# Local attention with channel mix: straight weight reads and every second PSUM column in the first unit's fp32 products

## The chip, the cores and the metric

The kernel runs on one core of one Trainium2 chip. The metric is the device time of one execution in microseconds (us). Before the change it is 390.84 us, the median of three runs (390.59 to 391.21).

## The reference

A local attention (chunks of 32 queries, each with 56 neighbouring keys and 8 memory keys, 4 batches, 8 heads, 768 positions, 64 values a head) is followed by a channel mix. Only the second part is touched by the change; its input `x` is the attention's output with 512 features per token.

```python
def _moe_ref(x, mu_k, mu_r, w_k, w_v, w_r):
    x_prev = ...                       # x, shifted by one token
    xk = mu_k * x + (1.0 - mu_k) * x_prev
    xr = mu_r * x + (1.0 - mu_r) * x_prev
    k = np.maximum(xk @ w_k, 0.0)      # 512 -> 1024
    v = k * k @ w_v                    # 1024 -> 512
    r = 1.0 / (1.0 + np.exp(-(xr @ w_r)))   # 512 -> 512
    return (r * v).astype(np.float32)
```

## The kernel before

The 4 x 768 tokens are cut into 12 units of 256 tokens, numbered `u`, and each unit into two tiles of 128 tokens, numbered `c`. For a unit the matrix engine (TensorE, in the profile PE) computes the scores `s`, transposes the probabilities into `pt`, multiplies them with the values into `px`, and then does the three products of the channel mix: `ph` (with `w_k`), the gate `pr` (with `w_r`) and `pv` (with `w_v`). The vector engine (DVE) and the scalar engine (ACT) do everything between the products.

The weights come from memory as 64-bit words in chunks `w0` to `w9` (`raw`). ACT and DVE turn each into a single fp32 tile `w` (`f_abs`, `f_low`, `f_join`: L325, L328, L332), and later split that into a high and a low part of type fp32r, `wk`, `wr` or `wv` and `wl` (L271 or L273, and L345). From unit 1 on each product is a sum of three fp32r products: high x high, high x low, low x high (L952, L1026, L1125). The first unit comes while the weights are still on their way; there the products use the undivided fp32 tiles, without a split:

- `f_row` (L998): `ph` of unit 0, 256 or 128 columns a call;
- `f_gate` with `is_whole(u)` (L943): `pr` of unit 0, for each of the two tiles four calls of 512 columns;
- `f_s2` with `is_whole(u, half)` (L1112): the first half of the sum over the 1024 features in `pv` of unit 0, four calls of 512 columns for each tile. The second half of this sum is done in fp32r (L1125), into the same PSUM bank.

A call with fp32 operands stands in the profile as two matmul rows with a weight load each, so L943 has 2 x 4 x 2 = 16 rows and L1112 as many. What is called the weight in these products, `w`, is the streamed operand of TensorE; the activations (`xf`, `kf`) are loaded into the array.

The order on each engine is set ahead of time by a planner (`Plan`) from a table of costs (`PE_COST`, `FULL`, `BLOCK`) and due times (`te_order`), and issued in that order. Loads and stores are issued from the queue of the sync engine (SP).

The columns of `w_v` and `w_r` lie in memory sorted: first the 256 even columns, then the 256 odd ones (`paired`, on the host). Two helpers put them back in order in the product:

```python
def woven(a):
    return a.rearrange("p (t n) -> p n t", t=2)

def pairs(a):
    return a.rearrange("p (n t) -> p n t", t=2)
```

With `woven(w)` the streamed operand is read alternately from the two halves: element 0, 256, 1, 257 and so on. With `pairs(p)` the results go to columns 0, 1, 2, 3 and so on, side by side. `f_row` uses neither: it reads its columns and writes them straight through.

Of the kernel before, what the change touches and what calls it, by code (L numbers as in the profile page):

```python
# [16 lines left out]
P = 128  # L17
# [8 lines left out]
FT = DFF // P  # L26
# [23 lines left out]
def woven(a):  # L50

    return a.rearrange("p (t n) -> p n t", t=2)


def pairs(a):
    return a.rearrange("p (n t) -> p n t", t=2)
# [22 lines left out]
class Plan:  # L81
# [7 lines left out]
    def op(self, alts, fn, deps=(), new=(), use=(), due=1e9):  # L89
        fixed = isinstance(alts, tuple)  # L90
        if fixed:
            alts = [alts]
        o = Op([(a + (False,))[:3] for a in alts], fn, deps, new, use, due)
        o.seq, o.fixed = len(self.ops), fixed
        self.ops.append(o)
        return o
# [121 lines left out]
def local_attention__then__channel_mix(  # L218
# [22 lines left out]
    def sb(tag, shape, name, dt=F32):  # L241
        return work.tile(shape, dt, tag=tag, name=name, bufs=bufs.get(tag, 1))

    def ps(tag, name, n=1):
        return psA.tile([P, n * 512], F32, tag=tag, name=name, bufs=bufs[tag])
# [21 lines left out]
    T = {}  # L267
# [109 lines left out]
    def wdeps(hl, ks):  # L377
        return [o for k in ks for o in wdone[id(hl[0]), k]]

    def word_deps(hl, ks):  # L380
        return [whole[id(hl[0]), k][0] for k in ks], [whole[id(hl[0]), k][1] for k in ks]

    def is_whole(u, half=0):
        return u == 0 and half == 0
# [550 lines left out]
    def channel_mix(u):  # L935
        b, t0 = units[u]

        def f_gate(c):
            p = T["pr", u, c] = ps("m", f"pr{u}_{c}")
            if is_whole(u):  # L940
                for k in range(KT):
                    w = T["w", id(wr_hl[0]), k // 2][:, k % 2 * DM : (k % 2 + 1) * DM]
                    nc.tensor.matmul(  # L943
                        pairs(p), T["xf", u, 1][:, k, c * P : (c + 1) * P], woven(w),
                        start=(k == 0), stop=(k == KT - 1),
                    )
                return
            xh, xl = T["xh", u, 1], T["xl", u, 1]
            wh, wl = ([w[k // 2][:, k % 2 * DM : (k % 2 + 1) * DM] for k in range(KT)] for w in wr_hl)
            for k in range(KT):  # L950
                for n, (x, w) in enumerate(((xh, wh[k]), (xh, wl[k]), (xl, wh[k]))):
                    nc.tensor.matmul(  # L952
                        pairs(p), x[:, k, c * P : (c + 1) * P], woven(w),
                        start=(k + n == 0), stop=(k == KT - 1 and n == 2),
                    )
# [13 lines left out]
        for c in range(QPU):  # L969
            grp.append(  # L970
                op(
                    ("pe", FULL if is_whole(u) else BLOCK), lambda c=c: f_gate(c),
                    grp[-1:] + (list(mix[u, 1][0].values()) if is_whole(u) else list(mix[u, 1][:2])) + wr,
                    new=[gs[c]], use=list(mix[u, 1][2:]) + wr_use, due=due["g", u, c],
                )
            )
# [41 lines left out]
        for f in range(FT // 2):  # L1018
# [14 lines left out]
            if f % 2 == 0:  # L1033
                kf = Slot(f"kf{z}")
# [64 lines left out]
        for c in range(QPU):  # L1099
            s = Slot("m")  # L1100
            prev = None
            for half in range(2):
                fs = range(FT // 4 * half, FT // 4 * (half + 1))

                def f_s2(c=c, half=half, fs=fs):
                    if half == 0:
                        T["pv", u, c] = ps("m", f"pv{u}_{c}")
                    p = T["pv", u, c]
                    if is_whole(u, half):
                        for f in [2 * f2 + i for f2 in fs for i in range(2)]:  # L1110
                            w = T["w", id(wv_hl[0]), f // 2][:, f % 2 * DM : (f % 2 + 1) * DM]
                            nc.tensor.matmul(  # L1112
                                pairs(p), T["kf", u, f // 4][:, f % 4, c * P : (c + 1) * P], woven(w),
                                start=(f == 0), stop=False,
                            )
                        return
                    for f2 in fs:
                        for i in range(2):
                            f = 2 * f2 + i
                            wh, wl = (w[f2][:, i * DM : (i + 1) * DM] for w in wv_hl)  # L1120
                            kh = T["kh", u, f2][:, i]
                            kl = T["kl", u, f2][:, i]
                            tc_ = slice(c * P, (c + 1) * P)
                            for n, (x, w) in enumerate(((kh, wh), (kh, wl), (kl, wh))):
                                nc.tensor.matmul(  # L1125
                                    pairs(p), x[:, tc_], woven(w), start=(f + n == 0), stop=(f == FT - 1 and n == 2)
                                )

                deps, use = [prev], []
                for f in fs:  # L1130
                    deps += ks[f][:2]
                    use += ks[f][2:]
                if is_whole(u, half):
                    wd, wd_use = word_deps(wv_hl, fs)
                    deps += wd
                    use += wd_use
                else:
                    deps += wdeps(wv_hl, fs)
                dv = due["v", u, c, half]
                prev = op(("pe", FULL if is_whole(u, half) else BLOCK), f_s2, deps, new=[s] if half == 0 else [], use=use + ([s] if half else []), due=dv)  # L1140
                if u == 0:
                    first_v.append(prev)
                if u == FAST - 1:
                    last_v.append(prev)

            def f_o(c=c):
                o = T["o", u, c] = sb("o", [P, DM], f"o{u}_{c}")
                p, sg = T["pv", u, c], T["sg", u][:, c * DM : (c + 1) * DM]
                nc.vector.tensor_mul(o, p, sg)

            def f_st(c=c):
                nc.sync.dma_start(out[b, t0 + c * P : t0 + (c + 1) * P, :], T["o", u, c])

            os = Slot("o")
            o_o = op(("dve", 0.62), f_o, [prev, o_g[c]], new=[os], use=[s, sgs], due=dv + BLOCK + 2)
            op(("dma", 0.75), f_st, [o_o], use=[os], due=dv + BLOCK + 6)
# [16 lines left out]
    with tc.manual_schedule():  # L1173
        for o in plan.order():
            if o.eng == "pe":
                n = 0 if ("ph", 0, 0) in T else int((o.start - busy - 0.2) / (0.43 if busy else 0.86))
# [56 lines left out]
```

## Time and profile before

| what | value |
|---|---|
| median of three runs | 390.84 us (390.59 to 391.21) |
| the profiled execution | 390.65 us |
| span of its profile | 388.5 us |
| busy DVE, ACT | 319.1 us (82%), 221.4 us (57%) |
| rows of L943 and L1112 | 16 and 16, 700 to 803 ns each |
| where they stand | 33.2 to 53.6 us of the span |

PE is the matrix engine, PEld its weight loads, SPq the queue from which transfers are issued. A matmul row's length is modelled and reaches into the next row, so what a row costs in a stream of rows is the distance of its start from the next one's start. In rows of the timeline the first number is the start, the second the length, both in us; in brackets behind a row stands how long its engine had been idle and what ended that.

### The profile page before, as it was taken

To read this page: it belongs to the slowest core of one execution; us is meant where nothing else is said; L and a number is where in the kernel's file an instruction comes from. 1 tells how busy PE (TensorE), PEld (TensorE's weight loads), DVE (VectorE), ACT (ScalarE), POOL (GpSimd) and SP (SyncE) were. 2 spreads that over 40 slices of the span, in tenths; PEclk is the share of its full clock that TensorE was granted. 3 is DMA by queue.
4 is the path that set the end of the run, shared out by engine and by line. 5 is a ranking of instruction groups with operands and counts; after the bars stand their busy time and mean duration, and the time that the engine had idled before them with its cause. 6 is when DMAs were issued, how large, how long until landed. Compare 5 with 4: busy or idle time off the path is not lost.

```text
span 388.5 us, 10736 instructions
## 1 busy us (share of the span) xinstructions
PE 382.2 (98%) x4776; PEld 351.8 (91%) x4776; DVE 319.1 (82%) x510; ACT 221.4 (57%) x329; POOL 2.8 (1%) x13
## 2 busy tenths in 40 slices
PE   8899999999999999999999999999999999999996
PEld 6785469988999999999999999999999999999996
DVE  3989798999899699699699689789779869969264
ACT  1789764955654464465466376267267356568260
POOL 2000000000000000000000000000000000000000
PEclk9999999999999999999999999999999999999999
DMA  8999683050042144134134134124134120000101
GB/s 318 420 392 417 251 280 128 29 164 29 27 158 118 54 126 149 54 114 162 54 112 164 57 110 164 56 110 164 56 108 167 56 87 24 30 29 2 54 2 54
DMA packets 13053, 48.98 MB, mean 126 GB/s; under 512 B 1488, under 2 KB 1872, under 8 KB 12496
## 3 DMA queue, kind: packets, MB, share of 16 engines
q1 hardware_dynamic: 13008, 48.31, 33.4%
q8 instruction: 37, 0.61, 0.7%
q14 instruction: 8, 0.07, 0.1%
HBM read 42.01 MB, written 6.29 MB: 124 GB/s over the span
## 4 chain that ended last, share of the span: by engine, by line
PE 97%; DVE 1%; issue 0%; ACT 0%; DVEq 0%
PE ph L1026 31%; PE pr L952 15%; PE accy L856 10%; PE accz L856 7%; PE accx L856 7%; PE px L526 6%; PE s L429 4%; PE pv L1125 4%; PE ph L998 4%; PE pt L509 3%; PE pv L1112 2%; PE pr L943 2%; PE warm L1179 1%; DVE mx L442 0%; DVE e L447 0%
## 5 line engine op out<-in xcount | busy, mean ns | idle before, releaser
L1026 PE MATMUL ph<-xh,wk 128*128 128x256 f32 x352 | 98.4, 280 | 0.0
L1026 PE MATMUL ph<-xl,wk 128*128 128x256 f32 x352 | 96.8, 275 | 0.0
L1026 PE MATMUL ph<-xh,wl 128*128 128x256 f32 x352 | 96.8, 275 | 0.0
L1045 ACT ACTIVATE kf<-ph 128x512 f32<-128x512 f32 x48 | 28.6, 598 | 75.9 <-PE ph L1026 75.8
L1026 PEld LDWEIGHTS ph<-xh,wk 128*128 128x128 f32 x352 | 67.5, 192 | 0.7
L1026 PEld LDWEIGHTS ph<-xl,wk 128*128 128x128 f32 x352 | 67.6, 192 | 0.1
L1026 PEld LDWEIGHTS ph<-xh,wl 128*128 128x128 f32 x352 | 67.6, 192 | 0.0
L273 DVE COPY aTz<-pt 64x512 f32<-64x512 f32 x20 | 13.8, 692 | 28.3 <-PE pt L509 19.1
L952 PE MATMUL pr<-wr,xh 128*128 128x512 f32 x88 | 34.5, 392 | 0.0
L801 DVE TENSOR_TENSOR al<-kf,ah 128x512 fp32r<-128x512 f32 x50 | 33.5, 684 | 0.4
L952 PE MATMUL pr<-wl,xh 128*128 128x512 f32 x88 | 33.4, 379 | 0.0
L952 PE MATMUL pr<-wr,xl 128*128 128x512 f32 x88 | 33.4, 379 | 0.0
L453 ACT ACTIVATE e<-e 128x1024 f32<-128x1024 f32 (+1 forms) x13 | 12.9, 993 | 33.1 <-DVE e L447 33.0
L526 PEld LDWEIGHTS px<-aTz,vw 128*64 128x64 f32 x768 | 23.5, 138 | 4.2 <-issue 1.8
L526 PE MATMUL px<-aTz,vw 128*64 128x64 f32 x768 | 25.2, 224 | 1.1 <-issue 1.1
L271 ACT CAST ah<-kf 128x512 fp32r<-128x512 f32 x40 | 24.9, 623 | 1.8 <-DVE kf L779 1.2
L1052 ACT ACTIVATE kf<-kf 128x512 f32<-128x512 f32 x40 | 25.2, 632 | 0.9
L271 ACT CAST xh<-df 128x1024 fp32r<-128x1024 f32 x11 | 16.4, 1491 | 14.6 <-DVE df L617 14.6
L856 PE MATMUL accx<-wv,ah 128*128 128x256 f32 x80 | 22.0, 275 | 0.0
L856 PE MATMUL accx<-wl,ah 128*128 128x256 f32 x80 | 22.0, 275 | 0.0
L856 PE MATMUL accx<-wv,al 128*128 128x256 f32 x80 | 22.0, 275 | 0.0
L961 ACT ACTIVATE sg<-pr 128x512 f32<-128x512 f32 x24 | 14.4, 609 | 10.6 <-PE pr L952 10.5
(125 smaller groups left out, 945.0 us busy)
## 6 DMA issues: line engine op xcount, KB each, us to landing
qk<-in_qk_dram SPq DMA_DIRECT2D x24, 768.0 KB, 5.9
vw<-in_vw_dram SPq DMA_DIRECT2D x24, 512.0 KB, 4.9
out_dram<-o SPq DMA_DIRECT2D x23, 256.0 KB, 2.0
raw<-in_w_k_dram SPq DMA_DIRECT2D x4, 1024.0 KB, 12.6
raw<-in_w_v_dram SPq DMA_DIRECT2D x4, 1024.0 KB, 8.9
raw<-in_w_r_dram SPq DMA_DIRECT2D x2, 1024.0 KB, 7.8
out_dram<-o SPq DMA_DIRECT2D x2, 128.0 KB, 1.7
id_sb<-in_ident_dram SPq DMA_DIRECT2D x1, 64.0 KB, 5.6
```

Of the source, the lines that this page charges most:

```text
L271: e.copy(dst, src)
L429: nc.tensor.matmul(s5[CHUNK * j : CHUNK * (j + 1), h, d - c, r, :], q4[z, r, j, :], k4[z, r, j, :], start=True, stop=True,)
L526: nc.tensor.matmul(p3[64 * h : 64 * h + 64, 2 * g : 2 * g + 2, CHUNK * j : CHUNK * j + CHUNK], v[:, g, h, j, :], a[:, h, g, j, :], start=True,
L801: nc.vector.tensor_sub(low(n), place[n](), T["ah", u, n].bitcast(F32))
L856: nc.tensor.matmul(o, x, w, start=(n in fresh and c + i == 0), stop=(c == cs[-1] and i == 2), skip_group_check=True)
L952: nc.tensor.matmul(pairs(p), x[:, k, c * P : (c + 1) * P], woven(w), start=(k + n == 0), stop=(k == KT - 1 and n == 2),)
L961: nc.scalar.activation(sg, p, AF.Sigmoid)
L998: nc.tensor.matmul(p[:, i * UTOK + c * P : i * UTOK + (c + n) * P], T["w", id(wk_hl[0]), k][:, fc], T["xf", u, 0][:, k, z], start=(i + k + ...
L1026: nc.tensor.matmul(pairs(p[:, i * UTOK : (i + 1) * UTOK]), w[:, fc], x[:, :, k].rearrange("p t n -> p n t"), start=(k + n == 0), stop=(k = ...
L1045: e.activation(part(), p, AF.Relu)
L1052: e.activation(q, q, AF.Square)
L1125: nc.tensor.matmul(pairs(p), x[:, tc_], woven(w), start=(f + n == 0), stop=(f == FT - 1 and n == 2))
```

## The change

Two helpers are added. `halves` reads an operand's first 256 columns and then its other 256, that is straight through. `apart` addresses the result's columns 0, 2, 4 up to 510 and then 1, 3, 5 up to 511. The two fp32 products of unit 0 that used `pairs` and `woven` use these instead. The result is the same at each column, since both sides are permuted alike.

```diff
+def halves(a):
+    return a.rearrange("p (t n) -> p t n", t=2)
+
+
+def apart(a):
+    return a.rearrange("p (n t) -> p t n", t=2)
...
                     nc.tensor.matmul(
-                        pairs(p), T["xf", u, 1][:, k, c * P : (c + 1) * P], woven(w),
+                        apart(p), T["xf", u, 1][:, k, c * P : (c + 1) * P], halves(w),
                         start=(k == 0), stop=(k == KT - 1),
                     )
...
                             nc.tensor.matmul(
-                                pairs(p), T["kf", u, f // 4][:, f % 4, c * P : (c + 1) * P], woven(w),
+                                apart(p), T["kf", u, f // 4][:, f % 4, c * P : (c + 1) * P], halves(w),
                                 start=(f == 0), stop=False,
                             )
```

A third place in the diff only breaks a line. The order of the instructions is the same on every engine before and after; behind the new helpers the line numbers grow by eight (L943 becomes L951, L1112 becomes L1120).

More of the change, by code (lines that the diff above doesn't have):

```diff
@@ L1125, in f_s2 @@
                                 nc.tensor.matmul(
-                                    pairs(p), x[:, tc_], woven(w), start=(f + n == 0), stop=(f == FT - 1 and n == 2)
+                                    pairs(p), x[:, tc_], woven(w),
+                                    start=(f + n == 0), stop=(f == FT - 1 and n == 2),
                                 )
```

## Prediction

> **What bounds the kernel now.** I read the page's first two parts first, for the busy engines, then the chain that ended last.
>
> ```profile
> PE 382.2 (98%) x4776; PEld 351.8 (91%) x4776; DVE 319.1 (82%) x510; ACT 221.4 (57%) x329; POOL 2.8 (1%) x13
> PEclk9999999999999999999999999999999999999999
> PE 97%; DVE 1%; issue 0%; ACT 0%; DVEq 0%
> ```
>
> The matrix engine (PE) is busy for 382.2 of 388.5 us, its granted clock is full in every slice, and 97% of the chain is PE work. A busy PE can still be a PE that waits now and then, so I read next what PE waited for, over the whole span. These are all rows of that view:
>
> ```profile
> PE warm L1179 <- DVE zero_sb L260: 1.2, 1, 1.2
> PE px L526 <- issue: 1.1, 2, 0.6
> PE s L429 <- issue: 0.3, 1, 0.3
> PE pt L509 <- DVE e L463: 0.2, 1, 0.2
> ```
>
> The waits sum to 2.8 us. A matmul that gets shorter therefore shortens the kernel, as long as what follows it on PE has its inputs early enough. I checked this below, because the edited matmuls run early (33 to 54 us), where the vector engine (DVE) is busy too.
>
> Third, the stage itself: pieces of the chain in order of time (start, length, what).
>
> ```profile
> 21.78 7.10 PE ph L998 x32
> 29.67 3.65 PE ph L998 x16
> 33.32 8.64 PE pr L943 x16
> 41.96 0.87 PE pt L509 x8
> 42.83 4.32 PE pv L1112 x8
> 47.15 2.02 PE px L526 x64
> 49.16 4.51 PE pv L1112 x8
> 53.68 1.41 PE s L429 x89
> 55.09 5.38 PE pv L1125 x24
> 79.45 2.59 PE pv L1125 x12
> ```
>
> The pieces touch one another: there is no hole on PE from 21.78 to 60.47 us. The edited lines are L943 (16 rows) and L1112 (8 + 8 rows). Their busy time is no price, since pipelined matmuls overlap (a row is shown with 703 ns below), so I price by spacing: 8.64 / 16 and 4.32 / 8 both give **0.540 us** for one row. The piece of 4.51 us is the same with a slower first row behind px.
>
> **The change part by part.** It moves nothing: the engines' instructions stand in the same order before and after, and the planner's costs are untouched. The 32 rows remain 32 rows with the same weights and the same 512 columns. Only two address patterns differ: the streamed operand is read straight through, and the result goes to every second PSUM column, first the even and then the odd ones.
>
> ```profile
> L943 PE MATMUL pr<-w,xf x16: 700/703/703, 33.2 to 41.3; 128*128 128x512 f32 x16
> L1112 PE MATMUL pv<-w,kf x16: 701/703/803, 42.7 to 53.0; 128*128 128x512 f32 x16
> L998 PE MATMUL ph<-xf,w x80: 275/379/483, 17.1 to 32.9; 128*128 128x256 f32 x48, 128*128 128x128 f32 x32
> ```
>
> *The read.* What does a row cost when an fp32 operand is read straight? L998 shows it: it is fp32, reads straight and writes side by side, with 256 columns. The difference of its two pieces removes the first row's start: (7.10 - 3.65) / 16 = 0.2156 us for 256 columns. Two such make 512 columns: **0.431 us**. The edited rows take 0.540, so the alternating read appears to cost 0.109 us each. The alternating read does not cost everywhere: L1125 reads alternately too, but in fp32r, and does 512 columns in 2.59 / 12 = 0.216 us, half of what straight fp32 takes per column. So the cost, if it is the read's, belongs to fp32 only. In the Trainium skill, "SBUF — State Buffer", section Specifications (TRN2), each crossing to a new 16-byte line pays. By that rule L1125 would have to be slow as well, which its 0.216 us contradicts, while L1112 fits it; I therefore do not build on the rule.
>
> *The write.* No row of this trace writes every second column, so the price has to be bounded. From below: two times L998 is the straight fp32 rate and 2 x 0.216 = 0.432 us is twice the fp32r rate. The two agree, and no row here does fp32 faster; the floor is 0.431 us. From above: adjacent columns share an aligned pair of words. L1125 writes 512 side-by-side columns in 0.216 us, which is one new pair every 0.84 ns. The new fp32 rows at 0.431 us would write one column every 0.84 ns, each in a new pair: exactly the rate of new pairs that PSUM takes from L1125 already. If instead fp32 goes over all columns twice at the fp32r rate, it asks for a new pair every 0.42 ns, twice of what any row shows, and a row could take 2 x 0.431 = 0.862 us. I take the floor, 0.431, since the pair rate that it needs is one that the trace shows and the other is not needed unless fp32 runs as two full sweeps.
>
> *The sum.* 32 x (0.540 - 0.431) = 3.49 us less on PE: 1.74 in L943, 0.87 in each half of L1112.
>
> *What is late next.* Work that stands behind the edited rows now starts up to 3.49 us sooner. Its inputs come from DVE and ACT, so I read when they are ready.
>
> ```profile
> 37.28 1.21 DVE L463 TENSOR_TENSOR e<-e,sum 128x1024 f32<-128x1024 f32 x1
> 38.41 2.35 DVE L332 SCALAR_TENSOR_TENSOR w<-w,raw 128x1024 uint32<-128x1024 uint32 x2
> 42.87 0.68 DVE L273 COPY aTz<-pt 64x512 f32<-64x512 f32 x1 [2.10 <-PE pt L509]
> 56.38 1.53 DVE L633 TENSOR_TENSOR xl<-xf,xh 128x1024 fp32r<-128x1024 f32 x1
> 60.50 0.69 DVE L1149 TENSOR_TENSOR o<-pv,sg 128x512 f32<-128x512 f32 x1 [0.86 <-PE pv L1125]
> 66.18 1.22 DVE L457 TENSOR_REDUCE sum<-e 128x16 f32<-128x1024 f32 x1 [0.69 <-ACT e L453]
> 70.21 1.22 DVE L633 TENSOR_TENSOR xl<-df,xh 128x1024 fp32r<-128x1024 f32 x1
> 71.34 1.22 DVE L345 TENSOR_TENSOR wl<-w,wr 128x1024 fp32r<-128x1024 f32 x1
> ```
>
> The transposes (pt) would start at 41.96 - 1.74 = 40.22 and need e, ready at 38.49. The first L1112 row would start at 41.1 and needs the weight joins, over at 40.76 (both of them; its first two rows use only the earlier). DVE itself stood idle for 2.10 us until pt came, so its work behind 42.87 also moves, by 1.74 us. At 60.50 it waited for pv, and at 66.18 for the exp of ACT:
>
> ```profile
> 63.18 0.60 ACT L1045 ACTIVATE kf<-ph 128x512 f32<-128x512 f32 x1 [7.89 <-PE ph L1026]
> 60.41 0.28 PE L1026 MATMUL ph<-xl,wk 128*128 128x256 f32 x1
> 72.33 0.38 PE L952 MATMUL pr<-wr,xl 128*128 128x512 f32 x1
> 73.41 0.38 PE L952 MATMUL pr<-wl,xh 128*128 128x512 f32 x1
> ```
>
> The first use of xl (60.41) has 60.41 - 57.91 = 2.50 us in hand now; with PE 3.49 ahead and DVE 1.74 ahead 0.75 is left. Thereafter DVE finds pv and exp ready sooner (ACT waited 7.89 us for PE alone, so it moves with PE) and gains the 0.86 and up to the 0.69: it is about 1.74 + 0.86 + 0.69 = 3.29 ahead. The next tight places are unit 1's gate: xl is ready at 71.43 for the row at 72.33 (0.90 in hand), wl at 72.56 for the row at 73.41 (0.85). Those need DVE at least 3.49 - 0.85 = 2.64 ahead, and it is 3.29. So I charge no wait. The queries for the scores at 53.68 would be wanted at 50.2; the transfers in this stage (one digit a microsecond, from 20 to 60 us) run dry well before that:
>
> ```profile
> DMA  9999999999999999999999994100078798587998
> 33.80 6.21 SPq L404 DMA_DIRECT2D qk<-in_qk_dram  x2
> ```
>
> The two loads were issued by 40.01 and the DMA engines fall idle at 46. From there on PE waits for nothing, so it carries the whole 3.49 us to the end. The profiled execution took 390.65 us, 2.15 more than its span and 0.19 below the median 390.84: 390.65 - 3.49 = **387.2 us**.
>
> **The rivals.** *PSUM takes the scattered writes more slowly than the read gains* (slower). For: no row shows such a write, and contiguous fp32r proves only a pair every 0.84 ns. The place is the same 32 rows, and the point from which it decides is a row of 0.540 us, a new pair every 1.05 ns. With one fp32r step (0.216 / 512 = 0.42 ns) more per column a row takes 0.431 + 0.216 = 0.647: +32 x 0.107 = +3.4, 394.1 us. With every column at double price (0.862), +32 x 0.322 = +10.3, 401.0 us. Against: fp32 needs two fp32r steps for each column, so the write has time for a new pair. The rule for this rival stands in the Trainium skill, "PSUM — Partial Sum Buffer", section Specifications (TRN2): lines of 8 bytes, and any pattern that is not contiguous slows matmuls significantly. No trace of this case shows it yet, nor whether it holds for fp32's slower columns. *The read order is not what costs* (no change). L998 differs from the edited lines in more than the read: 256 columns, not 512, and its calls change the bank while L943 stays on one for eight rows. If one of these makes the 0.540, or if the writes cost just what the read gave, the time stays at 390.65. Against: L1125 holds one bank with 512 columns and shows no loss. *DVE falls behind.* If DVE gained only the 1.74 us, the rows at 72.33 and 73.41 would wait 0.85 to 0.9 and the time would be 388.1; what I read of its idle times speaks against it.
>
> **How the numbers follow.** Forecast 387.2: chance 0.60, its own range 386.7 (an edited row a little below the floor, as a start is paid once for 512 columns) to 388.2 (DVE late). No change: 0.13. Slower: 0.27, about half of it near 394.1 and half near 401. The range from 386.7 to 394.4 holds the first two and the milder half of the third, 0.86; leaving the milder half out too would leave 0.27 outside. Within 0.2% (0.8 us) is about what a measurement of this kernel cannot tell from no change: faster 0.61, same 0.12, slower 0.27.
>
> **What would show it.** In the changed kernel's chain the pr piece with 16 rows at about 33.3 us should take 6.9 us in place of 8.64 and the two pv pieces about 3.5; the matmul rows should fall from 703 to near 594 ns. Rows above 703 ns make the scattered write the cost; rows at 703 say the read was not. PE's waits should still sum to about 2.8 us; a new row under them with DVE's xl or wl makes DVE the next bound. If the edited rows become shorter and the time does not, my reading of the slack is wrong.

## The result and the profile after

| | before | after |
|---|---|---|
| median | 391.05 us (6 runs, 390.59 to 391.57) | 387.60 us (6 runs, 387.16 to 388.02) |
| ratio | | 0.9912, 95% interval 0.9899 to 0.9925 |
| profiled execution, its span | 390.65 us, 388.5 us | 388.02 us, 385.9 us |

The kernel is 3.45 us faster by the medians, 0.9%. The page after the change shows the same machine at work: PE is busy for 98%, at full granted clock, and the chain is PE again.

```profile
PE 379.8 (98%) x4776; PEld 352.5 (91%) x4776; DVE 318.7 (83%) x510; ACT 221.5 (57%) x329; POOL 2.8 (1%) x13
PE 97%; DVE 1%; issue 0%; ACT 0%; DVEq 0%
```

What PE waited for over the whole span, after the change, again in full. Nothing new has come; the row for `s` at the start is gone.

```profile
PE warm L1188 <- DVE zero_sb L268: 1.2, 1, 1.2
PE px L534 <- issue: 1.1, 2, 0.6
PE pt L517 <- DVE e L471: 0.2, 1, 0.2
```

The stage itself, as pieces of the chain in order of time (start, length, what). L951 and L1120 are the edited lines, L1006 is `f_row`.

```profile
18.11 3.77 PE ph L1006 x32
22.67 7.10 PE ph L1006 x32
30.56 3.65 PE ph L1006 x16
34.21 6.87 PE pr L951 x16
41.95 3.44 PE pv L1120 x8
47.41 3.63 PE pv L1120 x8
52.45 5.38 PE pv L1133 x24
57.83 10.72 PE ph L1034 x96
```

The three edited pieces took 8.64 + 4.32 + 4.51 = 17.47 us before and take 6.87 + 3.44 + 3.63 = 13.94 now, 3.53 less, while `f_row`'s pieces of 7.10 and 3.65 have kept their length. A row costs 6.87 / 16 = 0.429 us in place of 0.540. The rows themselves, by form:

```profile
L951 PE MATMUL pr<-w,xf x16: 592/592/592, 34.0 to 40.5; 128*128 128x512 f32 x16
L1120 PE MATMUL pv<-w,kf x16: 592/593/697, 41.8 to 50.4; 128*128 128x512 f32 x16
```

The two profiled executions differ by only 2.63 us, not 3.5. That is not the change: in the one after, `f_row` began at 18.11 us, 0.90 later than before (17.21), and the edited rows come only behind it; 2.63 + 0.90 is the 3.53 of the pieces. Of the 0.90, 0.57 stand in the first warm-up rows and 0.33 in the scores behind them, which the change does not touch; a profile of an experiment that has the old read order began late as well (below, E2). What lengthens this start is not shown.

```profile
1.18 4.64 PE L1188 MATMUL warm<-zero_sb 128*128 128x256 f32 x10 [1.18 <-DVE zero_sb L268]
```

The same row of before, in its timeline, and the first piece of `f_row` in its chain:

```profile
1.18 4.07 PE L1179 MATMUL warm<-zero_sb 128*128 128x256 f32 x10 [1.18 <-DVE zero_sb L260]
17.21 3.78 PE ph L998 x32
```

### The profile page after: what moved, and what is told of

The parts are those of the page before. It is cut to its first block, busy times and chain, and to the rows that moved or that the text cites. A ratio compares the mean times of both kernels' runs of the same rounds, so it can differ in the third digit from the quotient of the medians.

```text
span 385.9 us, 10736 instructions
## 1 busy us (share of the span) xinstructions
PE 379.8 (98%) x4776; PEld 352.5 (91%) x4776; DVE 318.7 (83%) x510; ACT 221.5 (57%) x329; POOL 2.8 (1%) x13
## 4 chain that ended last, share of the span: by engine, by line
PE 97%; DVE 1%; issue 0%; ACT 0%; DVEq 0%
PE ph L1034 31%; PE pr L960 15%; PE accy L864 10%; PE accz L864 7%; PE accx L864 7%; PE px L534 6%; PE s L437 4%; PE pv L1133 4%; PE ph L1006 4%; PE pt L517 3%; PE pv L1120 2%; PE pr L951 2%; PE warm L1188 2%; DVE mx L450 0%; DVE e L455 0%
```

## The experiments

Each experiment starts from the changed kernel and replaces the address patterns of some matmuls. The theories that the expectations name: **A**, the alternating read alone cost 0.109 us a row; **B**, the side-by-side write after such a read cost it, and scattering the write cured it; **C**, both patterns cost something; **D**, the cost belongs to 512 columns on one bank. A word is one fp32 value of 4 bytes; a run of words is four neighbours, 16 bytes, counted from the start of the operand. In the cuts of code, `...` stands for what is left out. The kernel before, measured beside E1 to E4, had a median of 391.43 us (19 runs). E4, E5, E9 and E6 were executed once each, and up to 1 us of an execution is decided by its start, so they are read by their pieces and not by their totals.

**E1, straight read, side-by-side write.** Is the scattered write needed, or does it cost?

```diff
-    apart(p), ..., halves(w),
+    halves(p), ..., halves(w),
```

> The 32 edited rows read the weights straight and write side by side (the columns of unit 0's r and of the first half of its v come out sorted by halves, not in order). Theory A, the alternating read alone cost 0.109 us a row and the scattered write is free: rows stay 0.429 to 0.431 us apart and the time stays near 387.6 us. Theory B, it was the side-by-side write after an alternating read of 512 columns on one bank that cost, and scattering the write cured it: rows go back to 0.540, time near 391.05. Theory C, the scattered write costs a little that straight reading more than pays: rows fall below 0.429.

Measured: 387.9 us median, ratio to before 0.9910 (0.9894 to 0.9927). The pieces of the chain:

```profile
34.13 6.87 PE pr L951 x16
41.87 3.43 PE pv L1120 x8
47.32 3.63 PE pv L1120 x8
```

They equal those of the changed kernel to 0.01 us. So the scattered write costs nothing against a side-by-side one, and C falls. For the time it is not needed; it is there to put the columns in their order.

**E2, alternating read, scattered write.** The other half of the change alone.

```diff
+def apart4(a):
+    return a.rearrange("p (n t a) -> p a n t", t=2, a=2)
+def woven4(a):
+    return a.rearrange("p (t a n) -> p a n t", t=2, a=2)
...
-    apart(p), ..., halves(w),
+    apart4(p), ..., woven4(w),
```

> The 32 edited rows read alternately from the two halves, as before the change, and write every second column, as after it (unit 0's columns of r and v come out permuted). Theory A: rows 0.540 us apart, time near 391.05. Theory B: rows 0.429, time near 387.6. Theory C, both patterns cost: rows above 0.540, by 0.1 us each some 3 us more, near 394.

Measured: 391.34 us, ratio 1.0000 (0.9991 to 1.0009).

```profile
34.06 8.64 PE pr L959 x16
43.57 4.32 PE pv L1128 x8
49.90 4.51 PE pv L1128 x8
```

These are the pieces of before to the hundredth, though the write is scattered. B falls: the whole gain belongs to the read. The stage began late here as well (34.06 against 33.32 in the profile of before), since `f_row` began 0.75 us later.

**E3, the alternating read where it had not been.** `f_row` reads 256 or 128 columns a call, on changing banks.

```diff
-    p[:, i * UTOK + c * P : i * UTOK + (c + n) * P], T["w", id(wk_hl[0]), k][:, fc],
-    T["xf", u, 0][:, k, z],
+    pairs(p[:, i * UTOK + c * P : i * UTOK + (c + n) * P]), T["w", id(wk_hl[0]), k][:, fc],
+    woven(T["xf", u, 0][:, k, z]),
```

> The change stays, and unit 0's first product (f_row, 48 rows of 256 and 32 of 128 fp32 columns on changing banks), which read straight before and after, reads alternately from the two halves of its columns (tokens of unit 0 come out permuted within the product). Theory A, it is the alternating read whatever the length and the bank: rows of 256 columns go from 0.2156 to 0.270 us, rows of 128 from about 0.118 to 0.145, together 48 x 0.054 + 32 x 0.027 = 3.5 us, time near 391. Theory D, the cost belongs to 512 columns on one bank: rows unchanged, near 387.6.

Measured: 391.37 us, ratio to before 1.0002 (0.9991 to 1.0012), so the gain is gone again.

```profile
17.51 4.58 PE ph L1006 x32
22.88 8.93 PE ph L1006 x32
32.60 4.56 PE ph L1006 x16
37.16 6.87 PE pr L951 x16
```

The difference of the second and third piece gives (8.93 - 4.56) / 16 = 0.273 us for 256 columns, 0.058 more than straight; all three pieces together are 0.81 + 1.83 + 0.91 = 3.55 us longer. So the cost does not need 512 columns on one bank, and D falls.

**E4, which property of the order costs.** The gate alternates between neighbouring runs of four words; v reads 0, 2, 1, 3 within a run.

```diff
+def lines(a):
+    return a.rearrange("p (m t k) -> p m k t", t=2, k=4)   # gate
+def inline(a):
+    return a.rearrange("p (m k t) -> p m t k", k=2, t=2)   # v
...
-    apart(p), ..., halves(w),
+    inner(p), ..., lines(w),       # gate; inner writes side by side
...
-    apart(p), ..., halves(w),
+    inner2(p), ..., inline(w),     # v; inner2 writes side by side
```

> What about the read order costs? Writes side by side throughout. The gate's 16 rows alternate between neighbouring runs of four words (0, 4, 1, 5, 2, 6, 3, 7, then 8, 12 and so on); the 16 rows of v read within one run of four words in the order 0, 2, 1, 3 (columns of unit 0's r and v permuted). If leaving an aligned run of 16 bytes at each element costs: gate rows 0.540, v rows 0.431. If it is the distance of the two halves (1 KB): both 0.431. If it is any step other than to the next word: both 0.540. Time 387.6 to 391.

Measured: 388.86 us.

```profile
33.24 8.69 PE pr L967 x16
42.80 3.44 PE pv L1136 x8
48.25 3.63 PE pv L1136 x8
```

The gate's rows are 0.543 us apart, those of v 0.430. Neither the distance of 1 KB nor a step other than one is needed for the cost; leaving a run of 16 bytes at each word is enough. By itself E4 does not rule out that the size of the step decides (one or two words in v, three or four in the gate); E9 below speaks on that.

**E5, more and fewer changes of run.** Two words from each half in turn (gate), and every fourth word (v).

```diff
+def twos(a):
+    return a.rearrange("p (t n k) -> p n t k", t=2, k=2)   # gate
+def fourth(a):
+    return a.rearrange("p (n k) -> p k n", k=4)            # v
...
-    apart(p), ..., halves(w),
+    twos_out(p), ..., twos(w),     # gate; twos_out writes side by side
...
-    apart(p), ..., halves(w),
+    quarters(p), ..., fourth(w),   # v; quarters writes side by side
```

> After the runs before, one fp32 word on its own in an aligned run of four words costs 0.109 us over 512 columns. Writes side by side. The gate's 16 rows read two words from one half, two from the other (0, 1, 256, 257, 2, 3 and so on); the 16 rows of v read every fourth word (0, 4, 8 up to 508, then 1, 5, 9 and so on), so that each word lies in another run and none returns soon (columns of unit 0's r and v permuted). Theory A1, each change of run costs: gate 0.485 us a row (half as many changes), v 0.540. Theory A2, two words in a run hide the change, one does not: gate 0.431, v 0.540. Theory A3, only going back and forth between two places costs: gate 0.485 to 0.540, v 0.431.

Measured: 395.29 us; one execution of the kernel before is on record with it, at 390.65.

```profile
33.59 7.25 PE pr L967 x16
41.72 7.20 PE pv L1136 x8
50.93 7.37 PE pv L1136 x8
```

The gate's rows are 0.453 us apart: between A1's 0.485 and A2's 0.431, nearer to A2. Those of v are 0.900 us apart, which none of the three had: 0.47 more than straight, over four times what the alternating read costs. Going back and forth between two runs is thus the mild form; a new run for each word, not returned to soon, is the dear one. This is one pattern only: whether the missing return or the constant step of 16 bytes makes it so dear was not separated. The price of a change is not a constant, so A1 does not hold as it was put, and A2 holds only roughly.

**E9, two words of each run, and a write over 1 KB.** The gate reads every second word; v writes alternately to the two halves of its bank.

```diff
+def evens(a):
+    return a.rearrange("p (n k) -> p k n", k=2)
...
-    apart(p), ..., halves(w),
+    evens_out(p), ..., evens(w),   # gate; evens_out writes side by side
...
-    apart(p), ..., halves(w),
+    woven(p), ..., pairs(w),       # v; pairs reads straight
```

> The gate's 16 rows read every second word (0, 2, 4 up to 510, then 1, 3 and so on; two words of each run of four, writes side by side). The 16 rows of v read straight and write alternately to the two halves of the bank (0, 256, 1, 257), 1 KB apart, in place of every second column (columns of unit 0's r and v permuted). Theory A1: gate 0.485 us a row; A2: 0.431. Scattered writes are free for fp32 at any distance: v 0.430; a pair of words left open helps PSUM only for near writes: v above 0.430, up to 0.862.

Measured: 387.57 us; with it stands the same execution of before, 390.65.

```profile
33.40 7.20 PE pr L959 x16
41.47 3.44 PE pv L1128 x8
46.92 3.63 PE pv L1128 x8
```

Gate rows at 0.450 us confirm the 0.453 of E5: two words in a run take away most of the price, not all of it. A step of two words costs here, where every second one leaves its run, and cost nothing in E4's v, where it stays inside; and 256 words away (E5) or one run on (E9) makes 0.453 or 0.450. So it is the leaving of the run that counts, not the size of the step. The rows of v stay at 0.430: for plain fp32 a scattered write is free at 1 KB too.

**E6, straight reading in fp32r.** Does the alternating read cost the other products as well?

```diff
-    pairs(p), x[:, k, c * P : (c + 1) * P], woven(w),
+    halves(p), x[:, k, c * P : (c + 1) * P], halves(w),
```

> The change stays, and the fp32r gate of units 1 to 11 (264 rows of 512 columns, 0.216 us apart with the alternating read) reads the weights straight and writes side by side (columns of r permuted in those units). If the read order costs nothing in fp32r: rows 0.216 us apart, time 387.6. If the alternating read has a hidden price there too: rows below 0.216, and 264 times the difference less in all. If the alternating read is what makes 0.216 possible: rows above it, 0.01 us each being 2.6 us in all.

Measured: 392.42 us, beside the same 390.65 of before, so some 4.8 us slower than the median of the changed kernel.

```profile
69.14 2.80 PE pr L960 x12
73.95 3.00 PE pr L960 x12
80.95 5.80 PE pr L960 x24
```

The same pieces in the changed kernel:

```profile
69.42 2.59 PE pr L960 x12
74.03 2.79 PE pr L960 x12
80.82 5.38 PE pr L960 x24
```

A straight fp32r row costs 0.21 / 12 = 0.0175 us more, about 0.233 in place of 0.216. Over 264 rows that makes 4.6 us. The sign is the opposite of fp32's; why, no run here shows. What a scattered write does to fp32r was not tried on the chip, so the idea that the write is free because fp32 takes two fp32r steps for a column is argued only.

## Why the prediction held

- **The price of a row.** The spacing was taken from the chain (0.540), the straight rate from L998 doubled (0.431). Measured: 0.429; the small rest may be the start of a row, which would be paid once for 512 columns and twice in the doubling (not measured by itself). The sum of 3.49 us came out as 3.53 in the pieces and 3.45 in the medians; the forecast was 387.2 and the median is 387.6, with the median of before now 391.05, not the 390.65 of the profiled execution on which the sum was made: 391.05 - 3.49 = 387.56. The prediction's list of pieces leaves out one of the scores, from 28.88 to 29.67 us; with it the pieces touch, as the prediction says.
- **The read as the cause.** This was inferred from rows that differed in more than the read. E1, E2 and E3 together show it: the read alone, in both directions, at other lengths and on other banks.
- **The write at its floor.** The least certain choice, between 0.431 and 0.862. E1 and E9 show no cost. No row of before could decide it, and the reason given, the rate of new pairs, stays an argument; so that this part came out is in some measure luck.
- **The Trainium skill's rules.** "PSUM — Partial Sum Buffer", Specifications (TRN2), would have matmuls slow on any pattern that is not contiguous: here 0.429 us scattered and 0.429 side by side, so for plain fp32 the measurement speaks against it. "SBUF — State Buffer", the same section, asks for two hits on each line of 16 bytes: E4, E5 and E9 agree with it for plain fp32, nearly (0.450 to 0.453 with two words, 0.540 to 0.900 with one), while E6 shows the opposite for fp32r. The prediction had set this rule aside because of the fast fp32r rows; the runs say that the two types differ.
- **No new wait.** The slack was reckoned to shrink, not to vanish. Rows of the timelines of DVE and of PE after the change (start, length):

```profile
41.99 0.68 DVE L281 COPY aTz<-pt 64x512 f32<-64x512 f32 x1 [0.68 <-PE pt L517]
55.52 1.54 DVE L641 TENSOR_TENSOR xl<-xf,xh 128x1024 fp32r<-128x1024 f32 x1
63.60 1.21 DVE L465 TENSOR_REDUCE sum<-e 128x16 f32<-128x1024 f32 x1
67.62 1.22 DVE L641 TENSOR_TENSOR xl<-df,xh 128x1024 fp32r<-128x1024 f32 x1
68.76 1.22 DVE L353 TENSOR_TENSOR wl<-w,wr 128x1024 fp32r<-128x1024 f32 x1
```

```profile
57.77 0.28 PE L1034 MATMUL ph<-xl,wk 128*128 128x256 f32 x1
69.69 0.38 PE L960 MATMUL pr<-wr,xl 128*128 128x512 f32 x1
70.77 0.38 PE L960 MATMUL pr<-wl,xh 128*128 128x512 f32 x1
```

  The first use of xl has 57.77 - 57.06 = 0.71 us in hand (0.75 was reckoned), the gate 69.69 - 68.84 = 0.85 and 70.77 - 69.98 = 0.79 (0.90 and 0.85 before). DVE's sum starts at 63.60, 2.58 sooner, and 3.48 ahead once the late start of 0.90 is taken out; 3.29 was reckoned. DVE could follow because it had been waiting: its 2.10 us for pt fell to 0.68 (pt came 0.88 sooner, DVE's work before it ended 0.54 later), and its waits of 0.86 for pv and 0.69 for the exp are gone.
- **What would show it.** The pr piece was to take 6.9 us (6.87), the pv pieces about 3.5 (3.44 and 3.63), the rows 594 ns (592).

## What to carry to other kernels

Price a streamed matmul by the distance of its rows' starts, compare it with a row of the same type whose operands are plain, and look at the order in which its words are read before blaming the write. In plain fp32 move a permutation from the read to the PSUM write, where it cost nothing here; in fp32r leave the alternating read, which was the faster of the two here (0.216 against 0.233 us). When an engine bounds the kernel, follow the inputs of what it does next far enough to see whether the others wait for it: those waits are what lets them follow.

## What the runs showed of the hardware that was not expected

- 512 fp32 columns take 0.429 us read straight or within runs of four words, 0.450 to 0.453 with two words of a run at a time, 0.540 alternating between two runs, and 0.900 with each word in a new run.
- The fp32r gate prefers the opposite: 512 columns take 0.216 us alternating between two halves, 0.233 straight (E6).
- Every second column, or columns 1 KB apart, cost plain fp32 nothing on the PSUM side (0.429 and 0.430 us).
- The first ten warm-up rows, the same in all these kernels, took between 3.99 us (E9) and 4.64 us (the changed kernel, E6), and `f_row` began between 17.14 us (E4) and 18.11 us (the changed kernel): up to 1 us of an execution's time is decided before it. The granted clock there was 1.00 both in E4 and in the changed kernel; the cause is open.
- Start and pieces together give the profiled times. From the changed kernel's 388.02 us, the earlier start and the longer pieces make 388.87 us for E4 (388.86 measured), 395.28 for E5 (395.29) and 387.54 for E9 (387.57).
